# Two accumulator banks opened by real work, and the state tokens reordered so that one transfer stores 128 of them

## The chip, the cores and the metric

The kernel runs on one core of a Trainium2 chip. The metric is device time in microseconds (us) of one launch. A core has a matrix engine (TensorE, PE in the profile, its weight loads PEld), a vector engine (VectorE, DVE), a scalar engine (ScalarE, ACT), GpSimd (POOL) and SyncE (SP), which here only issues transfers. Each engine works through its own list of instructions in program order; semaphores tie the lists together. Matmul results land in PSUM, eight banks of 128 x 512 fp32.

## The reference

```python
# x: B=8, H=8, S=512, D=64; state: B, H, Ns=32, D; Dm = H*D = 512; E=8 experts, F=1024
a  = softmax(scale * x @ state.T);   xread = a @ state      # 512 rows per batch and head
a2 = softmax(scale * state @ x.T);   sread = a2 @ x         #  32 rows per batch and head
x  = concat([xread, sread], axis=2) -> (B*(S+Ns), H*D)      # 8 * 544 = 4352 tokens of 512
P  = exp(x @ w_gate - max);  8 times: P /= P.sum(1); P /= P.sum(0); P *= N / E
out = sum over e of P[:, e] * (relu(x @ w1[e]) @ w2[e])     # 4352 x 512, fp32
```

The order in which a kernel holds the tokens inside is free, as long as every row is stored at its place.

## The kernel before, in words

**Two stages.** Up to about 135 us the kernel computes the attention, expert 0, the gate and its eight normalisations, all as small operations whose order and engines stand in a list written out beforehand (PLAN, line 16, played by `issue`, line 105). After that a loop (lines 1039 to 1079) runs through experts 1 to 7. Both keep the running output in `acc`, 34 rows of 128 tokens x 512 columns in fp32.

**Token blocks.** Each expert has nine blocks: blocks 0 to 7 are the 512 x tokens of one batch, block 8 holds the 256 state tokens of all batches. `xsT` (line 165) holds the state tokens' inputs as 128 partitions x 4 chunks x 256 tokens; `keepS` (line 764) copies them there from PSUM, sixteen copies of 128 x 64, batch b at columns 32b to 32b+31. So a row of 128 state tokens in `acc` is four batches of 32, and `layer2_last` (line 299) stores it as four transfers of 32 rows, half of them from SP and half from ACT. The second of the two rows is computed in two halves of 256 columns.

**The loop.** One turn does layer 2 of a block (`layer2`, line 320) and, woven in, layer 1 of the next (`layer1`, line 263). Layer 2 is a seven-product scheme on a matrix cut in 2 x 2. The products go through PSUM in the order A, E, B, A, B, E, B, eight matmuls of 256 columns each; `add` (line 344) then puts a finished product into `acc`, weighted by P, as two DVE instructions of 128 x 256. The first A is also copied by ACT into the B bank (line 363), and the B products are added on top of it. The two B banks alternate from turn to turn. Layer 1 makes eight groups of 128 x 512 (two matmuls, line 255), which ACT passes through relu into `Hm` (line 275); after the fourth and the eighth group four DVE instructions form sums (lines 281 to 284), which the next turn's products read.

**Banks E and B also serve V.** For some turns, `project` (line 221) opens the turn with the V factors for later blocks: 24 small matmuls (line 235), the first into bank E and the turn's B bank. They wait until DVE has added what these banks held.

**The seeds.** In the first turn alone, `seed` (line 351) runs one matmul of 128 x 512 into each B bank, so that the later products, which never start a bank anew, add to it. What it writes is overwritten.

**The step counter.** `step` (line 1030) is called after each product and after each slot for a layer-1 group: 7 + 8 = 15 times a turn. Every sixth call advances `load_w` (line 188) by one, which first issues an expert's weight transfers and, 10 advances later, forms eight differences of its weights (line 206, eight DVE instructions of 128 x 512, called subs here), one at an advance. What is left of them when block 6 ends is emitted at once. So the position of a sub in DVE's list depends on the count alone; DVE's list is the program order of these calls.

**The turn's weighing.** Before the loop adds to `acc`, rows hold expert 0's unweighted result; `weigh` (line 292) multiplies a row by P. In the first turn, four rows are weighed on DVE, ACT, DVE and POOL.

Of the kernel before, what the change touches and what calls it, by code (L numbers as in the profile page):

```python
# [9 lines left out]
FP32 = mybir.dt.float32  # L10
FP16 = mybir.dt.float16
# [37 lines left out]
704V 689P 693P 690P 730P 398V 694A 399P 733P 731V 691A 732A 735A 734A 400V  # L49
""".split()  # L50
ENGINES = {"P": "PE", "V": "DVE", "A": "ACT", "G": "POOL", "D": "DMA", "S": "SPQ", "H": "HOST"}
NT_ = 2
ETX = 0
POOLB = 1
# [47 lines left out]
            slot.users.append(self)  # L102


def issue(ops):
    for step in PLAN:
        op = ops[int(step[:-1])]
        assert all(d.end for d in op.after) and ENGINES[step[-1]] in op.on
        for slot in op.takes:
            slot.ring.taken.append(slot)  # L110
            slot.tile = slot.make()
        op.emit(ENGINES[step[-1]])
        op.end = True
    assert all(op.end for op in ops) and len(PLAN) == len(ops)
# [3 lines left out]
def kernel(  # L118
# [9 lines left out]
    nc = tc.nc  # L128

    B, H, S, D = x.shape  # L130
# [30 lines left out]
    def bank(shape, dtype, name, tag="bank"):  # L161
        return pools[tag].tile(shape, dtype, name=name, tag=tag)
# [16 lines left out]
    w2r = moe_w2.rearrange("e (fb p) d -> e p fb d", p=128)  # L179

    outx = [out[b * SB:b * SB + S, :].rearrange("(p sc) d -> p sc d", sc=NSC) for b in range(B)]
    outs = out.rearrange("(b s) d -> b s d", s=SB)[:, S:, :]

    mw = ctx.enter_context(tc.tile_pool(name="moe_w", bufs=2))
    gsb = ctx.enter_context(tc.tile_pool(name="gate_sb", bufs=2))
# [72 lines left out]
    hid = {}  # L258
# [1 line left out]
    final = (E - 1, B)  # L260
    seeds = []

    def layer1(e, bi):

        t0, tn = blocks[bi]
        th = tn // 2
        Hm = hpool.tile([128, 2, NJ, S], FP16, name="Hm", tag="Hm")
        sm = hpool.tile([128, 3, NJ, S // 2], FP16, name="sm", tag="sm")
        hid[(e, bi)] = (Hm, sm)
        for j in range(NJ):  # L270
            for i in range(2):
                fb = i * NJ + j
                hps = bank([128, S], FP32, "hps", "h")
                hidden_ps(e, bi, fb, hps[:, :tn])
                nc.scalar.activation(out=Hm[:, i, j, :tn], in_=hps[:, :tn], func=AF.Relu)  # L275
                if j % 2 and i and (e, bi) != final:
                    def sums(jj=ds(j - 1, 2)):
                        a11, a21 = Hm[:, 0, jj, :th], Hm[:, 0, jj, th:tn]
                        a12, a22 = Hm[:, 1, jj, :th], Hm[:, 1, jj, th:tn]
                        s1, s2, s4 = (sm[:, k, jj, :th] for k in range(3))  # L280
                        nc.vector.tensor_add(s1, a21, a22)  # L281
                        nc.vector.tensor_sub(a21, a11, a21)  # L282
                        nc.vector.tensor_sub(s2, s1, a11)  # L283
                        nc.vector.tensor_sub(s4, a12, s2)  # L284

                    if DEFER and bi == 0 and j == 1:
                        late.append(sums)
                    else:
                        sums()
                yield  # L290
# [8 lines left out]
    def layer2_last():  # L299
        e, bi = final  # L300
        t0, tn = blocks[bi]
        Hm, _ = hid.pop(final)
        w2h = w16[e][1]
        nb = 128 // Ns
        for row in range(tn // 128):
            k = t0 // 128 + row
            parts = 1 + row
            for c in range(parts):
                cols = ds(c * (Dm // parts), Dm // parts)
                dst = bank([128, 512], FP32, "y", "AEh"[row + c])  # L310
                for fb in range(NFB):
                    nc.tensor.matmul(dst[:, :Dm // parts], Hm[:, fb // NJ, fb % NJ, ds(row * 128, 128)],  # L312
                                     w2h[:, fb, cols], start=(fb == 0), stop=(fb == NFB - 1))
                nc.vector.scalar_tensor_tensor(out=acc[:, k, cols], in0=dst[:, :Dm // parts], scalar=Pmat[:, k, e:e + 1],
                                               in1=acc[:, k, cols], op0=ALU.mult, op1=ALU.add)
            for i in range(nb):
                (nc.scalar if i % 2 else nc.sync).dma_start(
                    out=outs[row * nb + i], in_=acc[ds(i * Ns, Ns), k, :])

    def layer2(e, bi, n):  # L320
        t0, tn = blocks[bi]
        nk = tn // 256
        th = tn // 2
        Hm, sm = hid.pop((e, bi))
        w2h, T = w16[e][1], tsum[e]
        tb = t0 // 128
        p = Pmat[:, :, e:e + 1]
        A = bank([128, 2, DH], FP32, "A", "A")
        Eb = bank([128, 2, DH], FP32, "E", "E")

        def product(dst, lhs, rhs, first=False):
            for c in range(nk):
                for j in range(NJ):
                    nc.tensor.matmul(dst[:, c], lhs(j, c), rhs[:, j],  # L334
                                     start=first and c == 0 and j == 0, stop=(j == NJ - 1),
                                     skip_group_check=True)

        def h(i, half):
            return lambda j, c: Hm[:, i, j, ds(half * th + c * 128, 128)]

        def s(k):
            return lambda j, c: sm[:, k, j, ds(c * 128, 128)]

        def add(src, row, col):
            for c in range(nk):
                k = tb + row * nk + c
                dst = acc[:, k, ds(col * DH, DH)]
                nc.vector.scalar_tensor_tensor(out=dst, in0=src[:, c], scalar=p[:, k], in1=dst,  # L348
                                               op0=ALU.mult, op1=ALU.add)

        def seed(i):
            bb = bank([128, 2, DH], FP32, "Bseed", "B%d" % i)
            nc.tensor.matmul(bb.rearrange("p c d -> p (c d)"), identh, aT[:, 0, 0], start=True, stop=True)
            seeds.append(bb)

        if not n:
            for k, eng in enumerate(("DVE", "ACT", "DVE", "POOL")):
                weigh(k, eng)
        product(A, h(0, 0), w2h[:, :NJ, :DH], True)
        if not n:  # L360
            seed(0)
        Bb = seeds[n % 2]
        nc.scalar.copy(out=Bb[:, :nk], in_=A[:, :nk])  # L363
        yield
        product(Eb, s(0), T[:, 0], True)
        if not n:
            seed(1)
        add(Eb, 1, 1)
        yield
        product(Bb, s(1), T[:, 1])  # L370
        add(Bb, 0, 1)
        yield
        product(A, h(1, 0), w2h[:, NJ:, :DH])
        add(A, 0, 0)
        yield
        product(Bb, h(0, 1), T[:, 2])
        add(Bb, 1, 1)
        yield
        product(Eb, s(2), w2h[:, NJ:, DH:])
        add(Eb, 0, 1)  # L380
        yield
        product(Bb, h(1, 1), T[:, 3])
        add(Bb, 1, 0)
        if e == E - 1 and bi < B:
            for k in range(2 * nk):
                nc.sync.dma_start(out=outx[bi][:, k, :], in_=acc[:, tb + k, :])
        yield
# [179 lines left out]
    for b in range(B):  # L567
# [30 lines left out]
        for q in range(NQ):  # L598
# [163 lines left out]
                                             tile_position=(0, i * 64), skip_group_check=True)  # L762

            def keepS(eng, b=b, q=q, su=su):
                copy(eng, xsT[:, ds(2 * q, 2), ds(b * Ns, Ns)], su.tile)

            part("R%d" % (2 * b + q))
            u = op(r(9), {"PE": (0.26, 0.50)}, read, [k2], [su], [ETs, xn[b]])
# [246 lines left out]

                op((due_1 + 5.0 * bi, 2, j), {"DVE": (1.70, 1.85)}, sums, kept[-4:]).goal = -0.9

    issue(ops)
    for e in range(2):
        w16[e] = (wslots[e][0].tile, wslots[e][1].tile)  # L1020
    hpool = pools1["h"]
# [20 lines left out]
    for i, (e, bi) in enumerate(work):  # L1042
        if bi == 1 and e + 1 < E:
            wload.append(load_w(e + 1))
        if (e, bi) == final:
            layer2_last()
            break
        v, pat = iter(()), PATS if bi == B else PATN if bi == B - 1 else PAT0
        soon = work[:i + (3 if bi == B - 1 else 2)]
        need = sum(b < B for _, b in soon) * (F // 512)  # L1050
        if halves and all_halves - len(halves) < need:
            v, pat = project(halves[:SESSION], i), PATV
            del halves[:SESSION]
        if i:
            next(v, None)
        l2 = layer2(e, bi, i)
        l1 = layer1(*work[i + 1]) if i + 1 < len(work) and work[i + 1] not in hid else iter(())
        for k in range(7):
            next(l2)
            step()  # L1060
            if k == 0:
                next(v, None)
                next(v, None)
            if late:
                late.pop()()
            if e == 1 and bi < B and 3 <= k < 7:
                m = blocks[bi + 1][0] // 128 + k - 3
                if m < NTB:
                    weigh(m, "ACT")
            for _ in range(pat[k]):  # L1070
                next(l1, None)
                step()
        for part in (l1, l2):
            for _ in part:
                pass
        if bi == len(blocks) - 3:
            for _ in (x for w in wload for x in w):
                pass
            wload.clear()
# [30 lines left out]
```

## Time and profile before

| quantity | value |
|---|---|
| runs | 752.53, 752.74, 753.22 us; median 752.74 |
| profiled execution | 752.75 us, of which the span from first to last instruction is 751.0 |
| mean granted TensorE clock | 0.995 |
| busy PE / DVE / ACT / POOL | 736.0 / 617.0 / 517.7 / 70.8 us |
| seeds (line 353) | 2 matmuls, 379 ns each, at 136.0 and 137.3 us |
| subs (line 206) | 48 on DVE, about 415 ns each, from 191.0 to 649.6 us |
| stores of the state tokens (line 317) | 4 from SP, 4 from ACT, 64 KB each, issued from 746.1 to 748.0 us |

A matmul's time in the records overlaps the next one's: a run of matmuls of 512 columns starts one every 0.215 us, of 256 columns one every 0.109 us, whatever their own 0.38 and 0.27 us. In the timeline a line gives start, length, engine, source line, operation, result and operands, and how many instructions were merged; brackets hold the idle time before it.

### The profile page before, as it was taken

How to read it: one execution, taken by the hardware profiler on the slowest of the kernel's cores; microseconds unless marked ns; L12 is line 12 of the kernel's file. 1: busy time of each engine (PE TensorE's matmuls, PEld its weight loads, DVE VectorE, ACT ScalarE, POOL GpSimd, SP SyncE). 2: the span in 40 equal slices, each digit the busy share in tenths (PEclk: the TensorE clock that was granted, in tenths of full speed). 3: DMA queues.
4: the chain of work that ended last, by engine and by line, in shares of the span. 5: the costliest groups of instructions: out<-in, count | busy, mean ns of one | idle time of the engine just before them, and what ended most of it. 6: DMA issues, size and time to landing. Idle time of an engine off the chain costs nothing.

```text
span 751.0 us, 16151 instructions
## 1 busy us (share of the span) xinstructions
PE 736.0 (98%) x6517; PEld 502.2 (67%) x6517; DVE 617.0 (82%) x1529; ACT 517.7 (69%) x1014; POOL 70.8 (9%) x81
## 2 busy tenths in 40 slices
PE   5999999999999999999999999999999999999997
PEld 3444445666777777776776767776777767767776
DVE  5899989877888789788888788887897888887885
ACT  6876856799876766667666766667666676667662
POOL 4674410200010000100000000100001000000000
PEclk9899999999999999999999999999999999999999
DMA  9997560600033000700007000330007000002234
GB/s 179 140 134 131 82 99 1 109 6 1 1 61 53 2 1 2 113 1 2 1 2 112 2 1 1 58 57 1 1 2 112 2 1 2 1 31 94 103 113 141
DMA packets 51323, 36.71 MB, mean 49 GB/s; under 512 B 25392, under 2 KB 43824, under 8 KB 51248
## 3 DMA queue, kind: packets, MB, share of 16 engines
q0 software_dynamic: 22272, 20.97, 18.5%
q1 hardware_dynamic: 27744, 14.18, 7.6%
q8 instruction: 51, 0.84, 0.5%
q10 hardware_dynamic: 1232, 0.52, 0.3%
q14 instruction: 24, 0.20, 0.1%
HBM read 42.48 MB, written 8.91 MB: 68 GB/s over the span
## 4 chain that ended last, share of the span: by engine, by line
PE 92%; DVE 3%; DMA 1%; ACT 1%; POOL 1%; issue 0%; SPq 0%; POOLq 0%; DVEq 0%; ACTq 0%
PE hps L255 28%; PE Bseed L334 20%; PE A L334 14%; PE E L334 14%; PE yps L935 6%; PE hps L897 4%; PE v_ps L235 4%; DMA xT<-x_nat 1%; DMA x_nat<-in_x_dram 1%; PE y L312 0%; PE v_ps L870 0%; POOL a L670 0%; ACT Hm L275 0%; DVE acc L348 0%; POOL E L662 0%; PE su_ps L758 0%
## 5 line engine op out<-in xcount | busy, mean ns | idle before, releaser
L275 ACT ACTIVATE Hm<-hps 128x512 f16<-128x512 f32 (+1 forms) x496 | 265.8, 577 | 130.5 <-PE hps L255 128.1
L255 PE MATMUL hps<-aT,V 128*128 128x512 f16 x880 | 230.6, 379 | 0.0
L334 PEld LDWEIGHTS <-Hm 128*128 128x128 f16 x1888 | 181.6, 98 | 71.3 <-issue 15.9
L348 DVE SCALAR_TENSOR_TENSOR acc<-Bseed,Pmat,acc 128x256 f32<-128x256 f32 x354 | 155.0, 477 | 9.8 <-PE Bseed L334 6.9
L334 PEld LDWEIGHTS <-sm 128*128 128x128 f16 x1416 | 138.3, 98 | 34.5 <-issue 0.3
L334 PE MATMUL A<-w2h,Hm 128*128 128x256 f16 x944 | 123.7, 273 | 0.0
L334 PE MATMUL Bseed<-T,Hm 128*128 128x256 f16 x944 | 123.3, 273 | 0.0
L255 PEld LDWEIGHTS <-V 128*128 128x128 f16 x880 | 86.1, 98 | 50.8
L348 DVE SCALAR_TENSOR_TENSOR acc<-E,Pmat,acc 128x256 f32<-128x256 f32 x236 | 103.2, 476 | 13.8 <-PE E L334 13.5
L281 DVE TENSOR_TENSOR sm<-Hm 128x512 f16<-128x512 f16 (+1 forms) x122 | 50.1, 411 | 60.4 <-ACT Hm L275 60.2
L243 ACT CAST V<-v_ps 128x512 f16<-128x512 f32 x144 | 74.2, 612 | 0.0
L348 DVE SCALAR_TENSOR_TENSOR acc<-A,Pmat,acc 128x256 f32<-128x256 f32 x118 | 51.9, 479 | 17.9 <-PE A L334 17.6
L935 PE MATMUL yps<-w2h,hT 128*128 128x512 f16 x272 | 64.1, 379 | 0.1
L334 PE MATMUL E<-w2h,sm 128*128 128x256 f16 x472 | 61.7, 273 | 0.0
L334 PE MATMUL E<-T,sm 128*128 128x256 f16 x472 | 61.6, 273 | 0.0
L334 PE MATMUL Bseed<-T,sm 128*128 128x256 f16 x472 | 61.5, 272 | 0.0
L363 ACT COPY Bseed<-A 128x512 f32<-128x512 f32 (+1 forms) x62 | 34.1, 550 | 37.9 <-PE A L334 35.3
L282 DVE TENSOR_TENSOR Hm<-Hm 128x512 f16<-128x512 f16 (+1 forms) x122 | 50.3, 412 | 4.2
L284 DVE TENSOR_TENSOR sm<-Hm,sm 128x512 f16<-128x512 f16 (+1 forms) x122 | 50.2, 412 | 4.2
L283 DVE TENSOR_TENSOR sm<-sm,Hm 128x512 f16<-128x512 f16 (+1 forms) x122 | 49.4, 405 | 0.0
L194 POOL DMA_DIRECT2D w1h<-in_moe_w_dram x12 | 8.5, 714 | 396.9 <-PE hps L255 396.5
L935 PEld LDWEIGHTS <-hT 128*128 128x128 f16 x272 | 25.4, 99 | 28.9 <-issue 1.8
(127 smaller groups left out, 617.7 us busy)
## 6 DMA issues: line engine op xcount, KB each, us to landing
w1h<-in_moe_w_dram POOLq DMA_DIRECT2D x16, 512.0 KB, 7.0
w2h<-in_moe_w_dram POOLq DMA_DIRECT2D x16, 512.0 KB, 8.4
out_dram<-acc SPq DMA_DIRECT2D x32, 256.0 KB, 2.5
x_nat<-in_x_dram POOLq DMA_DIRECT2D x16, 256.0 KB, 5.6
st_st<-in_state_dram ACTq DMA_DIRECT2D x1, 256.0 KB, 4.9
st_st<-in_state_dram SPq DMA_DIRECT2D x1, 256.0 KB, 4.2
ETs<-E SPq DMA_TRANSPOSE x16, 4.3
out_dram<-acc SPq DMA_DIRECT2D x4, 64.0 KB, 1.8
```

The lines of the kernel that those rows point to most:

```text
L235: nc.tensor.matmul(ps[q][ds(j * Ns, Ns), :], stT[ds(r, 64), bi, q, ds((j ^ q) * Ns, Ns)], w1h[ds(r, 64), 2 * q + j // 2, cols], tile_posit ...
L243: nc.scalar.copy(out=dst, in_=src)
L255: nc.tensor.matmul(out, lhs, rhs, start=(k == 0), stop=(k == len(terms) - 1))
L275: nc.scalar.activation(out=Hm[:, i, j, :tn], in_=hps[:, :tn], func=AF.Relu)
L281: nc.vector.tensor_add(s1, a21, a22)
L282: nc.vector.tensor_sub(a21, a11, a21)
L283: nc.vector.tensor_sub(s2, s1, a11)
L284: nc.vector.tensor_sub(s4, a12, s2)
L334: nc.tensor.matmul(dst[:, c], lhs(j, c), rhs[:, j], start=first and c == 0 and j == 0, stop=(j == NJ - 1), skip_group_check=True)
L348: nc.vector.scalar_tensor_tensor(out=dst, in0=src[:, c], scalar=p[:, k], in1=dst, op0=ALU.mult, op1=ALU.add)
L363: nc.scalar.copy(out=Bb[:, :nk], in_=A[:, :nk])
L935: nc.tensor.matmul(yps.tile, hT[fb].tile[:, ds(tk * 128, 128)], w2h[:, fb, :], start=(fb == 0), stop=(fb == NFB - 1))
```

## The change

1. **First turn.** The seed matmuls go. Both B banks are allocated ahead of the turn. Layer 2 gets an extra stop after its first product, at which the first layer-1 group of the next block runs, into the B bank of this turn instead of a bank of its own (`lent`); relu empties it, and then the copy of A goes into it. The other B bank is first written by the V matmuls of the second turn. The rows are weighed in another order (2 on DVE, 3 on POOL, 0 on DVE, 1 on ACT behind the copy). The extra stop calls `step` once more.
2. **State tokens.** `keepS` writes batch b at every fourth column, so that a row of 128 tokens has the batch innermost; `layer2_last` stores the first row by one transfer (SP), and each half of the second row by one as soon as it is added (ACT, then SP).
3. `issue` gets a hook, `idle`, whose table `IDLE` is empty: nothing is emitted.

```diff
-    outs = out.rearrange("(b s) d -> b s d", s=SB)[:, S:, :]
+    nb = 128 // Ns
+    outs = out.rearrange("(g b s) d -> g s b d", b=nb, s=SB)[:, S:, :, :]
@@ layer1(e, bi, lent=None)
-                hps = bank([128, S], FP32, "hps", "h")
+                if lent is None:
+                    hps = bank([128, S], FP32, "hps", "h")
+                else:
+                    hps, lent = lent, None
@@ layer2_last
-            for i in range(nb):
-                (nc.scalar if i % 2 else nc.sync).dma_start(
-                    out=outs[row * nb + i], in_=acc[ds(i * Ns, Ns), k, :])
+                (nc.scalar if c + 1 < parts else nc.sync).dma_start(
+                    out=outs[row, :, :, cols], in_=acc[:, k, cols])
@@ layer2
-        def seed(i):
-            bb = bank([128, 2, DH], FP32, "Bseed", "B%d" % i)
-            nc.tensor.matmul(bb.rearrange("p c d -> p (c d)"), identh, aT[:, 0, 0], start=True, stop=True)
-            seeds.append(bb)
-
         if not n:
-            for k, eng in enumerate(("DVE", "ACT", "DVE", "POOL")):
+            for k, eng in ((2, "DVE"), (3, "POOL"), (0, "DVE")):
                 weigh(k, eng)
         product(A, h(0, 0), w2h[:, :NJ, :DH], True)
+        Bb = seeds[n % 2]
         if not n:
-            seed(0)
-        Bb = seeds[n % 2]
+            yield
         nc.scalar.copy(out=Bb[:, :nk], in_=A[:, :nk])
+        if not n:
+            weigh(1, "ACT")
         yield
         product(Eb, s(0), T[:, 0], True)
-        if not n:
-            seed(1)
         add(Eb, 1, 1)
@@ keepS
-                copy(eng, xsT[:, ds(2 * q, 2), ds(b * Ns, Ns)], su.tile)
+                copy(eng, xsT.rearrange("p c (g n b) -> p c g n b", g=B // nb, b=nb)[:, ds(2 * q, 2), b // nb, :, b % nb], su.tile)
@@ the loop
+        if not i:
+            seeds += [bank([128, 2, DH], FP32, "Bseed", "B%d" % k) for k in range(2)]
         l2 = layer2(e, bi, i)
-        l1 = layer1(*work[i + 1]) if i + 1 < len(work) and work[i + 1] not in hid else iter(())
+        l1 = iter(())
+        if i + 1 < len(work) and work[i + 1] not in hid:
+            l1 = layer1(*work[i + 1], None if i else seeds[0].rearrange("p c d -> p (c d)"))
+        if not i:
+            next(l2)
+            next(l1)
+            step()
         for k in range(7):
             next(l2)
             step()
```

More of the change, by code (lines that the diff above doesn't have):

```diff
@@ L51 @@
 ENGINES = {"P": "PE", "V": "DVE", "A": "ACT", "G": "POOL", "D": "DMA", "S": "SPQ", "H": "HOST"}
+IDLE = {}
 NT_ = 2
@@ L102, in __init__, with issue @@
             slot.users.append(self)
-def issue(ops):
+def issue(ops, idle):
     for step in PLAN:
@@ L111, in issue @@
             slot.tile = slot.make()
+        idle(op.takes[0].tile if op.takes else None, IDLE.get(int(step[:-1]), 0))
         op.emit(ENGINES[step[-1]])
@@ L261, with layer1 @@
     seeds = []
-    def layer1(e, bi):
+    def layer1(e, bi, lent=None):
         t0, tn = blocks[bi]
@@ L303, in layer2_last @@
         w2h = w16[e][1]
-        nb = 128 // Ns
         for row in range(tn // 128):
@@ L1016, with idle @@
                 op((due_1 + 5.0 * bi, 2, j), {"DVE": (1.70, 1.85)}, sums, kept[-4:]).goal = -0.9
-    issue(ops)
+    def idle(t, n):
+        if not n:
+            return
+        t = t.rearrange({2: "p a -> p a", 3: "p a b -> p (a b)", 4: "p a b c -> p (a b c)"}[len(t.shape)])[:, :128]
+        for _ in range(n):
+            if t.dtype == FP16:
+                nc.tensor.transpose(t, identh, identh)
+            else:
+                nc.tensor.matmul(t, identh, identh, start=True, stop=True, skip_group_check=True)
+    issue(ops, idle)
     for e in range(2):
```

## The prediction

> **What bounds the kernel now.** The page comes first: engines, then the chain that ended last.
>
> ```profile
> PE 736.0 (98%) x6517; PEld 502.2 (67%) x6517; DVE 617.0 (82%) x1529; ACT 517.7 (69%) x1014; POOL 70.8 (9%) x81
> ...
> PE 92%; DVE 3%; DMA 1%; ACT 1%; POOL 1%; issue 0%; SPq 0%; POOLq 0%; DVEq 0%; ACTq 0%
> ```
>
> PE bounds it: a matmul removed is time gained, and so is a wait of PE. But DVE at 82% over all hides a tight place in every turn, which the timeline shows. First a turn (expert 2, block 2) without a sub, then one (expert 5, block 5) with a sub of line 206 before the second E adds:
>
> ```profile
> 252.25 0.87 DVE L348 SCALAR_TENSOR_TENSOR acc<-Bseed,Pmat,acc 128x256 f32<-128x256 f32 x2
> 253.04 0.87 DVE L348 SCALAR_TENSOR_TENSOR acc<-E,Pmat,acc 128x256 f32<-128x256 f32 x2
> 253.19 1.04 PE L334 MATMUL Bseed<-T,Hm 128*128 128x256 f16 x8
> 254.93 0.28 PE L334 MATMUL A<-w2h,Hm 128*128 128x256 f16 x1
> ```
> ```profile
> 546.24 0.87 DVE L348 SCALAR_TENSOR_TENSOR acc<-Bseed,Pmat,acc 128x256 f32<-128x256 f32 x2
> 547.02 0.41 DVE L206 TENSOR_TENSOR T<-w2h 128x512 f16<-128x512 f16 x1
> 547.16 1.04 PE L334 MATMUL Bseed<-T,Hm 128*128 128x256 f16 x8
> 547.36 0.87 DVE L348 SCALAR_TENSOR_TENSOR acc<-E,Pmat,acc 128x256 f32<-128x256 f32 x2
> 549.05 1.05 PE L334 MATMUL A<-w2h,Hm 128*128 128x256 f16 x8
> ```
>
> The last B product starts 0.07 us after the B adds end (252.25 + 0.87 = 253.12), in the second turn 0.05: it overwrites what they read, and there is no slack. The sub puts the E adds off by 0.34 (547.36 - 547.02). The V matmuls behind the product need bank E empty, and so the next A starts 1.89 us after the last B product instead of 1.74.
>
> The first turn and the end, from the timeline:
>
> ```profile
> 135.14 1.05 PE L334 MATMUL A<-w2h,Hm 128*128 128x256 f16 x8
> 136.03 0.38 PE L353 MATMUL Bseed<-aT,identh 128*128 128x512 f16 x1
> 136.41 1.03 PE L334 MATMUL E<-T,sm 128*128 128x256 f16 x8
> 136.86 0.60 ACT L363 COPY Bseed<-A 128x512 f32<-128x512 f32 x1
> 137.28 0.38 PE L353 MATMUL Bseed<-aT,identh 128*128 128x512 f16 x1
> 137.93 1.04 PE L334 MATMUL Bseed<-T,sm 128*128 128x256 f16 x8
> ```
> ```profile
> 746.06 2.33 ACTq L317 DMA_DIRECT2D out_dram<-acc  x4
> 747.02 0.48 DVE L314 SCALAR_TENSOR_TENSOR acc<-y,Pmat,acc 128x256 f32<-128x256 f32 x1 [0.39 <-PE y L312]
> ```
> ```profile
> out_dram<-acc SPq DMA_DIRECT2D x32, 256.0 KB, 2.5
> ...
> out_dram<-acc SPq DMA_DIRECT2D x4, 64.0 KB, 1.8
> out_dram<-acc ACTq DMA_DIRECT2D x4, 64.0 KB, 2.0
> ```
>
> **Part 1, the seeds: -0.43.** Two matmuls of 512 columns go, 2 x 0.215 = 0.43 us of PE. The layer-1 group that comes forward is done once either way. What it risks is the copy: relu and copy now run one after the other before the first B product. The group starts where the seed did, 136.03, and ends by 136.62 (0.59, as line 255's pairs take); ACT is free at 136.35, its V casts done; relu 136.66 to 137.26, copy 137.29 to 137.88 (0.60 each), product at 137.93: the same moment as before, with a group more behind it. The V factors that it reads come from the first ACT cast, done about 135.3, and the DVE cast, 135.31. Nearest bounds: -0.25 if relu and copy come 0.18 later, -0.60 if the gap of 0.17 ahead of E (136.41 against 136.03 + 0.215) goes with no wait in its place. The weighing is covered: E's second add waits for POOL's row 3 until 138.05 as before; row 1, now behind the copy, is ready about 138.6, its adds come at 139.1. On ACT the next relu waits behind it until 138.6 instead of 138.19, and four layer-1 banks cover that. The fourth relu comes one place earlier, so the first turn's sums do too, and its last B product, 0.43 earlier, finds its bank free. The second bank needs no work: 24 V matmuls write it in the second turn anyway (145.41).
>
> **Part 2, the extra step: +1.87.** The first turn calls `step` 16 times instead of 15, and from then on every sub stands one place earlier in DVE's list. PE's list is otherwise untouched. By letters (adds E, B, A; sums S; sub T), the order in which the instructions stand is:
>
> ```
> expert, block   before        after          expert, block   before        after
> 1, 5            EBTASBTESB    ETBASTBESTB    4, 5            EBATSBETSB    EBATSBTESB
> 1, 6            TEBATSBETSB   EBTASBTESB     4, 6            ETBASBTESB    ETBASTBESTB
> 2, 5            EBATSBETSB    EBATSBTESB     5, 5            EBTASBTESB    ETBASTBESTB
> 2, 6            EBTASBTESB    ETBASTBESTB    5, 6            TEBATSBETSB   EBATSBTESB
> 3, 5            ETBASBTESB    ETBASTBESTB    6, 5            EBATSBETSB    EBTASBTESB
> 3, 6            TEBATSBETSB   EBATSBTESB     6, 6            EBTASBTESB    ETBASTBESTB
> ```
>
> - New is the pair S T B, a sub between the first sums and the second B adds, once an expert. No turn before has it. From the sums' start DVE runs without a pause (sums, B, E), so the sub's 0.34 goes onto the B adds, and the last B product waits for them. Slack, from the timeline: 0.01 to 0.02 where V matmuls opened the turn (253.19 against 253.12, less the 0.05 that is always there), 0.08 where not (340.69 against 340.56), none in expert 1, where ACT's weighing already keeps that product waiting (196.14; its layer-1 matmuls end at 195.19 + 0.86 = 196.05). So 0.34 (expert 1), 3 x 0.33 (experts 2, 5, 6), 2 x 0.27 (3, 4): 1.87.
> - T before the E adds costs only where V matmuls open the next turn: last B product to next A took 1.74 without (340.69 to 342.43), 1.83 with it (371.14 to 372.97), and 1.89 in the turn shown. Before, four turns pay: 3,5 and 4,6 0.09 each, 5,5 and 6,6 0.15 each, 0.48. After, these are S T B turns, where V starts later by more than the E adds do, and four others pay: 1,6 and 6,5 0.09, 2,5 and 3,6 0.15: 0.48 again. No change.
> - Subs at other places (B T A, A T S, E T B) lie in DVE's idle time: 0.36 us before the A adds, 1.16 before the sums.
> - Bounds: 0 if the sub slips in unseen, as those do; 2.35 if each S T B costs a sub's whole 0.42 less the slack (0.42 + 3 x 0.41 + 2 x 0.35). I take the 0.34 measured between the very neighbours B, T, E. POOL's list is unchanged, and the weight transfers are issued long before they are read.
>
> **Part 3, the end: -0.35.** Before, the last adds end at 747.50 (747.02 + 0.48); then each queue issues two transfers, the last from ACT at 748.0 with 2.0 us to landing, 750.0; 1.0 more to the span's end. After, one transfer of 128 KB follows the adds, from SP at 747.57. No row has 128 KB: between 1.8 (64 KB) and 2.5 (256 KB). By size 2.0; I take 2.1, since its runs are 1 KB: 749.65, -0.35. Bounds: -0.6 (1.8) and +0.1 (2.5). The first half's transfer leaves ACT about 746.7 and has landed by then. The Trainium skill speaks against such a gain: "DMA: Bandwidth & Descriptors", Anatomy of one DMA, gives 2.0 us fixed plus the bytes at 436 GB/s, here 2.3 us as an estimate. By that the part would bring 0.1 and the sum would be 754.1; the rows of 1.8 for 64 KB lie below the rule.
>
> **Part 4, the strided copies: 0.** Sixteen `keepS` copies of about 0.21 us now write every fourth element. Nearest row: the DVE reduction that reads its 272 values strided takes 0.65 against 0.44 in a row, +0.05 for 64 values. They end by 98.7 us; only the last two lead on, through the gate to P at 136.1, and the bank that waits for P's first adds is not written again for 4 us. So 0 to +0.3, and I take 0.
>
> **Sum.** 752.75 - 0.43 + 1.87 - 0.35 = 753.84, about 753.8. The profiled execution is within 0.01 of the median 752.74.
>
> **Rivals.**
> - *The sub stays hidden (ends faster).* If S T B costs the last B product nothing, because the sums start earlier than the rows say, only the gains are left: 752.75 - 0.43 - 0.35 = 751.97, and to 751.6 with the better bounds. It decides if the sum of the S T B waits is under 0.78. For it: the B, T, A and A, T, S subs do vanish. Against: the sums wait for ACT's relu, which nothing moves, and the slack was read as 0.01 to 0.08.
> - *The gains fail.* The copy keeps PE waiting at the first turn (-0.25), the last transfer lands like one of 256 KB (+0.1), a sub costs 0.42 at its six places (2.35): 752.75 - 0.25 + 0.1 + 2.35 = 754.95. For it: no row shows these sizes. Against: three bounds together.
> - *The change does not do what it says.* The list of PE shows both seeds gone, that of SP and ACT three stores instead of eight. There is no room for this one.
>
> **How the numbers follow.** Forecast, each part near its price: 0.66, 753.2 to 754.7. Sub hidden: 0.15, 751.3 to 752.8. Gains fail: 0.19, 754.3 to 755.3. The range 752.2 to 755.0 takes in the forecast, most of the third case and half of the second. A measurement here tells 0.2%, 1.5 us, from no change: 751.2 and 754.2. Above 754.2 lie the third case and a quarter of the forecast, 0.35; under 751.2 the tail of the second and what I overlook, 0.06; between them 0.59.
>
> **What would show it.** No line 353; the first B product still near 137.9; the next turn's V matmuls near 145.0 instead of 145.41. In the six S T B turns, a wait of PE for DVE of 0.27 to 0.34 ahead of the last B product, and the new line of subs between sums and B adds; these turns, from first A to next first A, 10.7 to 10.8 us long where V matmuls follow and 9.9 to 10.0 where not. The last store landing about 749.65 plus the shift. Wrong if these turns keep their length, if the last transfer takes 2.5 or more, or if anything before 135 us moves by more than 0.3.

## The result, and the profile after

The changed kernel takes 755.09 us (median of 17 runs, 753.66 to 756.85) where the kernel before takes 752.97 us (17 runs, 751.01 to 755.71): a ratio of 1.0026, 95% interval 1.0018 to 1.0034. On the 752.74 us of the forecast that ratio is 754.7 us. The forecast was 753.8, in a range of 752.2 to 755.0: a loss, as forecast, but nearly twice as large (+1.96 us instead of +1.09), and, with 0.26% (interval from 0.18%), past the 0.2% within which I had put the likeliest outcome.

When the first turn starts differs from run to run: two kernels with the same first part (the changed kernel, and the one without the extra step below) start it at 134.16 and at 135.77 us. So the prediction's sign of being wrong, that anything before 135 us moves by more than 0.3 us, tells nothing here. Two profiles are therefore compared from the first A product of the loop to the span's end, called the stretch here. It takes 615.83 us before (750.97 - 135.14) and 617.73 us after (751.89 - 134.16): +1.90, which is the difference in time within its interval (1.4 to 2.6 us). Turns are numbered from 0: turn n is expert 1 + n // 9, block n % 9.

The page of the changed kernel, its engines and the chain that ended last:

```profile
PE 735.7 (98%) x6515; PEld 501.1 (67%) x6515; DVE 616.8 (82%) x1529; ACT 518.6 (69%) x1014; POOL 70.7 (9%) x81
...
PE 88%; DVE 5%; ACT 3%; DMA 2%; POOL 1%; issue 0%; SPq 0%; POOLq 0%; ACTq 0%
```

PE has two matmuls fewer, and yet its share of the chain falls from 92% to 88%: DVE and ACT now stand where PE stood. This shift belongs to the moved subs: with the extra step alone the shares are 88% PE, 5% DVE and 3% ACT, and without it 92, 3 and 1%. A share of the chain is not the loss, which is 0.3% of the span. The costliest groups show two new waits of PE (busy time, mean ns, idle time ahead and what ended it), first after, then before:

```profile
L338 PE MATMUL Bseed<-T,Hm 128*128 128x256 f16 x944 | 123.3, 273 | 1.0 <-DVE acc L352 0.8
...
L338 PE MATMUL Bseed<-T,sm 128*128 128x256 f16 x472 | 61.6, 272 | 0.3
```
```profile
L334 PE MATMUL Bseed<-T,Hm 128*128 128x256 f16 x944 | 123.3, 273 | 0.0
...
L334 PE MATMUL Bseed<-T,sm 128*128 128x256 f16 x472 | 61.5, 272 | 0.0
```

The later B products (from `Hm`) now wait 1.0 us for DVE's adds, as forecast. The first B products (from `sm`) wait 0.3 us, which was not. Both are counted from the modelled ends of the matmuls ahead and so are too small; the lengths of the turns below have the whole of it. The timeline of the S T B turn of expert 5, block 5 (turn 41), whose counterpart of before the prediction shows:

```profile
546.46 0.42 DVE L209 TENSOR_TENSOR T<-w2h 128x512 f16<-128x512 f16 x1
546.52 1.03 PE L258 MATMUL hps<-aT,V 128*128 128x512 f16 x4
546.79 0.87 DVE L352 SCALAR_TENSOR_TENSOR acc<-Bseed,Pmat,acc 128x256 f32<-128x256 f32 x2
...
547.72 1.03 PE L338 MATMUL Bseed<-T,Hm 128*128 128x256 f16 x8 [0.17 <-DVE acc L352]
```

The sub stands between sums and B adds and puts them off by 0.33 (546.79 - 546.46). The four layer-1 matmuls, one every 0.215, are done at 547.38; the product starts at 547.72, 0.06 after the adds: a wait of 0.34. The turn takes 10.77 us instead of 10.59, because the next A came late before too (the E adds behind the sub). The first turn, in the same view:

```profile
134.16 1.05 PE L338 MATMUL A<-w2h,Hm 128*128 128x256 f16 x8
...
135.05 0.59 PE L258 MATMUL Bseed<-aT,V 128*128 128x512 f16 x2
...
135.68 0.60 ACT L281 ACTIVATE Hm<-Bseed 128x512 f16<-128x512 f32 x1 [0.30 <-PE Bseed L258]
...
136.31 0.57 ACT L362 COPY Bseed<-A 128x512 f32<-128x512 f32 x1
...
136.93 1.03 PE L338 MATMUL Bseed<-T,sm 128*128 128x256 f16 x8
```

The first B product starts 2.77 us after the first A (2.79 before), with a layer-1 group already done, and the next turn's V matmuls start 9.81 after it (143.97) instead of 10.27. The end, timeline and then the transfers (KB each, median us to landing):

```profile
747.99 0.48 DVE L319 SCALAR_TENSOR_TENSOR acc<-y,Pmat,acc 128x256 f32<-128x256 f32 x1 [0.39 <-PE y L317]
```
```profile
out_dram<-acc ACTq DMA_DIRECT2D x1, 128.0 KB, 2.3
out_dram<-acc SPq DMA_DIRECT2D x1, 128.0 KB, 2.1
```

SP finds the last store landed 2.15 us after the adds end at 748.47, where it was 2.46 before: 0.3 us gained. But the span ends 3.42 after the adds, and did so 3.46 after them before. All turns whose length differs by more than 0.05 us between the two profiles, first A to next first A:

| turn (expert, block) | before | after | difference |
|---|---|---|---|
| first turn (1,0) | 11.04 | 10.59 | -0.45 |
| S T B: 1,5 / 2,6 | 9.67 / 9.58 | 10.00 / 9.90 | +0.33, +0.32 |
| S T B: 3,5 / 4,6 / 5,5 / 6,6 | 10.52 / 10.52 / 10.59 / 10.58 | 10.70 / 10.70 / 10.77 / 10.77 | +0.18, +0.18, +0.18, +0.19 |
| T before the last E adds: 1,6 / 2,5 / 3,6 / 6,5 | 10.43 / 10.45 / 10.45 / 10.43 | 10.52 / 10.59 / 10.59 / 10.52 | +0.09, +0.14, +0.14, +0.09 |
| turns 29 (4,2) and 56 (7,2), without a sub | 9.58 / 9.58 | 9.86 / 9.87 | +0.28, +0.29 |

First turn -0.45, subs +1.84, turns 29 and 56 +0.57, the end -0.04; a few hundredths are rounding. Turns 29 and 56 have no sub and no moved instruction. In turn 29 the timeline shows what is late:

```profile
420.19 1.05 PE L338 MATMUL A<-w2h,Hm 128*128 128x256 f16 x8
...
421.61 0.57 ACT L362 COPY Bseed<-A 128x512 f32<-128x512 f32 x1 [0.65 <-PE A L338]
...
422.23 1.03 PE L338 MATMUL Bseed<-T,sm 128*128 128x256 f16 x8
```

The same turn before:

```profile
420.42 1.05 PE L334 MATMUL A<-w2h,Hm 128*128 128x256 f16 x8
...
421.56 0.57 ACT L363 COPY Bseed<-A 128x512 f32<-128x512 f32 x1 [0.36 <-PE A L334]
...
422.18 1.03 PE L334 MATMUL Bseed<-T,sm 128*128 128x256 f16 x8
```

ACT's copy of A starts 1.42 us after the A product does, 1.14 before, and the B product waits for it. In the trace's records ACT's semaphore wait ahead of the copy ends at 421.29, with the A product; the copy follows after 0.32 us, where this usually takes 0.04. Counted from 0 in ACT's records, semaphore waits included, the copy stands at place 703 of ACT's list in turn 29 and at 1087 in turn 56. Both leave 63 on division by 128. Before they stood at 704 and 1088: the new first turn has one semaphore wait fewer on ACT.

### The profile page after: what moved, and what is told of

It reads as the page before. It is cut to its first block, busy times and chain, and to the rows that moved or that the text cites. A ratio compares the mean times of both kernels' runs of the same rounds, so it can differ in the third digit from the quotient of the medians.

```text
span 751.9 us, 16140 instructions
## 1 busy us (share of the span) xinstructions
PE 735.7 (98%) x6515; PEld 501.1 (67%) x6515; DVE 616.8 (82%) x1529; ACT 518.6 (69%) x1014; POOL 70.7 (9%) x81
## 4 chain that ended last, share of the span: by engine, by line
PE 88%; DVE 5%; ACT 3%; DMA 2%; POOL 1%; issue 0%; SPq 0%; POOLq 0%; ACTq 0%
PE hps L258 26%; PE Bseed L338 20%; PE A L338 14%; PE E L338 12%; PE yps L934 6%; PE hps L896 4%; PE v_ps L238 4%; ACT Hm L281 2%; DMA xT<-x_nat 1%; DVE acc L352 1%; DMA x_nat<-in_x_dram 1%; PE su_ps L757 0%; PE y L317 0%; DVE sm L287 0%; DVE Hm L288 0%
```

## The experiments

Two theories stood against each other. Mine: the loss is the place of the subs, 1.84 us, plus 0.57 us for ACT's place in its list, while the stores' gain is used up behind the landing. The rival: the subs are hidden, and stores and first turn cost what is seen. All numbers below that are not ratios come from the profiles, one execution of each kernel.

| kernel | ratio to before (95%) | stretch, us | last adds to span's end, us |
|---|---|---|---|
| before | | 615.83 | 3.46 |
| after | 1.0026 (1.0018 to 1.0034) | 617.73 | 3.42 |
| without the extra step | 0.9994 (0.9983 to 1.0006) | 615.85 | 3.38 |
| extra step alone | 1.0030 (1.0017 to 1.0043) | 617.66 | 3.46 |
| tokens and stores alone | 1.0000 (0.9990 to 1.0010) | 615.77 | 3.41 |
| one more ACT instruction | 1.0020 (1.0009 to 1.0030) | 617.13 | 3.39 |
| 18 S T B pairs | one run, no ratio | 620.88 | 3.41 |
| six more stores | 1.0019 (1.0008 to 1.0031) | 617.32 | 3.02 |
| 128 / 101 / 86 more on ACT | one run each, no ratio | 617.68 / 617.73 / 617.16 | 3.42 / 3.41 / 3.42 |
| best of the parts | 0.9988 (0.9978 to 0.9997) | 614.50 | 3.05 |

**Without the extra step.**

```diff
             next(l2)
             next(l1)
-            step()
```

> The changed kernel without the additional step() in the first turn: subs stand where they stood before the change, everything else is the changed kernel's. All numbers from the first A product to the span's end (615.86 us before, 617.74 us after). Theory (the place of the subs costs 1.84 us): no S T B turn is left and the stretch shrinks by 1.84 us against the changed kernel, to about 615.9 us; the first turn stays at 10.6 us. Rival (the pairs S T B wait in the place of something else, and the loss comes from the new stores and the first turn): the stretch stays near 617.7 us. About turns 29 and 56, which are 0.28 us longer in the changed kernel: if ACT's position in its list does it, they stay 0.28 us longer, since ACT's list is the changed kernel's; if the moved subs do it, both go back to 9.58 us and the stretch is 615.3 us.

The stretch is 615.85 us, 1.88 less than in the changed kernel; all ten turns with subs have the lengths of before, the first turn stays at 10.59, turns 29 and 56 at 9.86 and 9.87. In turn 41 the sub is behind the B adds again (timeline):

```profile
546.68 0.87 DVE L352 SCALAR_TENSOR_TENSOR acc<-Bseed,Pmat,acc 128x256 f32<-128x256 f32 x2
...
547.46 0.41 DVE L209 TENSOR_TENSOR T<-w2h 128x512 f16<-128x512 f16 x1
547.61 1.04 PE L338 MATMUL Bseed<-T,Hm 128*128 128x256 f16 x8
```

The product no longer waits. One call, which adds no work, costs as much as the whole net loss; what is left of the other parts cancels (first turn -0.45, turns 29 and 56 +0.57, end -0.08). And since turns 29 and 56 are late without the moved subs, these are not their cause.

**The extra step alone.**

```diff
 # kernel before
-    n = 0
+    n = 1
```

> The kernel before with its step counter started at 1, so that every sub stands one place earlier, as in the changed kernel; the seeds, the token order and the stores are as before. Theory: six S T B turns, 0.18 us longer (three times, V matmuls next), 0.32 to 0.34 us longer (twice and once), four turns of 10.5 to 10.6 us take the places of four others, together +1.84 us: from the first A product to the span's end 617.7 us against 615.86 us. Rival (S T B is hidden without the other parts): 615.9 us. About turns 29 and 56: if ACT's position in its list makes them longer, they stay at 9.58 us here (ACT's list is that of the kernel before); if the moved subs do, both are 0.28 us longer and the stretch is 618.3 us.

617.66 us, +1.83, with the changed kernel's lengths in all ten turns (one 0.01 off) and 9.58 in turns 29 and 56. The place of the subs costs its 1.84 with the old first turn and the old stores just as well.

**Tokens and stores alone.** The kernel before with the new `keepS`, `outs` and `layer2_last` only.

```diff
-                copy(eng, xsT[:, ds(2 * q, 2), ds(b * Ns, Ns)], su.tile)
+                copy(eng, xsT.rearrange("p c (g n b) -> p c g n b", g=B // nb, b=nb)[:, ds(2 * q, 2), b // nb, :, b % nb], su.tile)
...
-            for i in range(nb):
-                (nc.scalar if i % 2 else nc.sync).dma_start(
-                    out=outs[row * nb + i], in_=acc[ds(i * Ns, Ns), k, :])
+                (nc.scalar if c + 1 < parts else nc.sync).dma_start(
+                    out=outs[row, :, :, cols], in_=acc[:, k, cols])
```

> The kernel before with the state tokens in the new order and the three stores alone; seeds, first turn and subs as before. Theory (the last store lands 0.33 us sooner, but SP then still steps through six semaphores at about 0.06 us each, where it stepped through one or two): from the last adds' end to the span's end 3.43 us against 3.50 us before, the stretch from the first A product 615.8 us, and the start of that stretch as far as runs scatter (0.3 us or more). Rival A (the end is worth the 0.35 us that I forecast): 615.5 us. Rival B (the strided copies of the tokens delay the first part): the stretch starts up to 0.3 us later than in runs of the kernel before.

3.41 us from the adds to the end: 0.05 gained, not 0.35. The loop starts at 135.07, within the scatter of the starts, and the ratio is 1.0000 within 0.1%: a cost of the strided copies above 0.75 us is excluded, a smaller one isn't resolved.

**One more ACT instruction.** The tiny activation that loads ACT's table, issued twice.

```diff
-lambda _: nc.scalar.activation(out=warm, in_=warm, func=AF.Exp), ops[-1:])
+lambda _: [nc.scalar.activation(out=warm, in_=warm, func=AF.Exp) for _ in range(2)], ops[-1:])
```

> The changed kernel with the tiny activation that loads ACT's table issued twice, so that all of ACT's list from there on stands one instruction later, as in the kernel before. Theory (turns 29 and 56 are 0.28 us longer because ACT's copy of A into B stands last in a block of 128 instructions of ACT's list, at 703 and 1087, and starts 0.28 us late there): both go back to 9.58 us and the stretch from the first A product to the span's end is 617.74 - 0.57 = 617.2 us. Rival (the data, the subs or the transfers at those times do it): both stay at 9.86 us and the stretch at 617.7 us.

Both turns are back at 9.58 us, and the stretch is 617.13, 0.60 less, with one instruction more. Turn 29 in the timeline:

```profile
420.49 1.05 PE L338 MATMUL A<-w2h,Hm 128*128 128x256 f16 x8
...
421.63 0.57 ACT L362 COPY Bseed<-A 128x512 f32<-128x512 f32 x1 [0.36 <-PE A L338]
...
422.25 1.03 PE L338 MATMUL Bseed<-T,sm 128*128 128x256 f16 x8
```

**128, 101 and 86 more.** Is it the place on division by 128, or would any shift do? Tiny copies behind the activation move all of ACT's list; the first part starts later by what they take (first A at 158.62, 156.66 and 149.68 us), which says nothing of the loop.

```diff
+[nc.scalar.activation(out=warm, in_=warm, func=AF.Exp)] + [nc.scalar.copy(out=warm, in_=warm) for _ in range(128)]
```

> The changed kernel with 128 additional tiny copies on ACT behind the activation that loads its table, so that all of ACT's list stands 128 instructions later; the first part starts later by what they take. Theory (the position in blocks of 128 instructions makes turns 29 and 56 longer): 128 is a whole block, so both turns are 9.86 us again, as in the changed kernel, and unlike with one additional instruction. Rival (any shift, or any delay of the first part, takes the 0.28 us away): both are 9.58 us.

> The changed kernel with 101 additional tiny copies on ACT ahead of the first part. In the changed kernel ACT's copies of A into B in turns 31 and 58 stand at 730 and 1114 of its list; here at 831 and 1215, both 63 on division by 128, with the semaphore wait at 62. Theory (a copy at 63, behind a semaphore wait at 62, starts 0.28 us late): turns 31 and 58 are 0.28 us longer than in the changed kernel, and turns 29 and 56 are back at 9.58 us. In turns 22 and 49 the copy stands at 65 here; by the theory they stay at 9.58 us, and a longer time there would say that the place is wider. Rival (turns 29 and 56 have something else of their own, such as a transfer at that time): they stay at 9.86 us, and 31 and 58 do not change.

> As the run with 101 additional copies, with 86: the copies of turns 14 and 41 then stand at 62 on division by 128 (574 and 958) with their semaphore wait at 61, those of turns 32 and 59 at 65, and none with a semaphore wait ahead of it at 63 or 64. Theory in its narrow form (only a copy at 63 is late): no turn is longer than in the changed kernel, and turns 29 and 56 are back at 9.58 us. Rival (the block's refill delays whatever stands just ahead of it): turns 14 and 41 are 0.28 us longer too.

With 128 more, turns 29 and 56 take 9.86 again. With 101 they take 9.58, and turns 31 and 58 take 10.72 instead of 10.44, with the copy 1.42 us after A once more (timeline of turn 31):

```profile
462.72 1.05 PE L338 MATMUL A<-w2h,Hm 128*128 128x256 f16 x8
...
464.14 0.57 ACT L362 COPY Bseed<-A 128x512 f32<-128x512 f32 x1 [0.65 <-PE A L338]
...
464.76 1.03 PE L338 MATMUL Bseed<-T,sm 128*128 128x256 f16 x8
```

Turns 22 and 49, at place 65, keep their 9.58. With 86 no turn is longer, though copies stand at 62 (turns 14 and 41) and at 65 (32 and 59). So for this copy it is place 63 alone, and only behind a separate semaphore wait: in the changed kernel's turns 20 and 47 no copy is late at 62, and in the kernel before one stands at 63 there with nothing ahead of it but an activation, and is not late. For other instructions the place is not enough: with 101 and with 86 more, two relus each stand at 63 directly behind a separate wait (575 and 959, 703 and 1087) and start 0.04 us after it, as usual.

**18 S T B pairs.** The dose: the same subs, three S T B turns an expert instead of one.

```diff
-        if n % 6 == 0 and wload:
+        if n % 5 == 3 and wload:
...
-            step()          # the one added in the first turn
```

> The changed kernel without the additional step(), and with the sub issued on every step() whose count leaves 3 on division by 5 (instead of every sixth): the 8 subs of an expert then stand in three turns, each of which has one pair S T B; 18 such pairs instead of the changed kernel's six, and no sub before the last E adds. Theory (each pair costs the 0.27 to 0.34 us by which the last B product waits): against the kernel without the additional step() 18 x 0.27 to 18 x 0.34 less the 0.48 us that its other subs cost, +4.4 to +5.6 us; from the first A product to the span's end 620.2 to 621.4 us. Rival (only the first such pair after a weight transfer costs, or the pairs cost by something else than their place): 617.7 us or less.

620.88 us: 5.03 above the kernel without the extra step, or 0.31 us a pair ((5.03 + 0.48) / 18). Its row of later B products, beside 1.0 in the changed kernel:

```profile
L338 PE MATMUL Bseed<-T,Hm 128*128 128x256 f16 x944 | 123.3, 273 | 2.8 <-DVE acc L352 2.1
```

**Six more stores.** Where does the gain of the earlier landing go? In the trace's records SP, once all is issued, steps through nine waits for transfers, always in the same order, and about 0.06 us apart when nothing holds it. The transfers take eight of these semaphores in turn. The changed kernel's last store has the third wait of the list. SP passes it at 750.62, and six more up to 750.98; before, the last store to land had the seventh (749.97).

```diff
-                nc.sync.dma_start(out=outx[bi][:, k, :], in_=acc[:, tb + k, :])
+                for c in ([ds(0, DH), ds(DH, DH)] if bi < 3 and k < 2 else [ds(0, Dm)]):
+                    nc.sync.dma_start(out=outx[bi][:, k, c], in_=acc[:, tb + k, c])
```

> The changed kernel with six of the x stores of the first three blocks of the last expert split into two halves each, some 80 us ahead of the end: six more transfers, so that the last store's semaphore is the last of SP's list instead of the third. Theory (after the landing SP steps through six more semaphores at 0.06 us each): the landing stays 2.1 us after the issue, and from the last adds' end to the span's end it is 3.42 - 0.36 = 3.06 us. Rival (the order does not matter, the stretch behind the landing is fixed): 3.4 us as in the changed kernel. Everything else as in the changed kernel.

3.02 us instead of 3.42: the last store's wait is now the last of the list. SP passes it at 751.12, 2.08 us after the store's issue (2.09 in the changed kernel), and the span ends 0.88 later instead of 1.26. The waits of SP at the end (us in all, times, longest), first in the changed kernel, then here:

```profile
SPq L1122 <- DMA out_dram<-acc: 1.4, 2, 0.7
```
```profile
SPq L1123 <- DMA out_dram<-acc: 1.0, 2, 0.7
```

The last landing holds SP 0.7 us in both; what comes behind it is what differs. Six transfers more made the end 0.4 us sooner in the profile; the ratios (1.0019 and 1.0026) are too close to show it.

**Best of the parts.** The changed kernel without the extra step, with subs at `n % 5 == 2`, one more ACT instruction and the six split stores.

```diff
-        if n % 6 == 0 and wload:
+        if n % 5 == 2 and wload:
```

> The seeds, the token order and the stores of the changed kernel, without the additional step(), with the sub on every step() whose count leaves 2 on division by 5 (pairs B T A... become A T S and E T S, all in DVE's idle time), one additional tiny ACT instruction, and the six split x stores. Theory, against the kernel before, from the first A product to the span's end: first turn -0.45, subs -0.48, end -0.40, turns 29 and 56 unchanged, together -1.33: 614.5 us, a ratio of 0.9982. Rival (E T S delays the sums and with them the last B product, as S T B did): no gain of 0.48 and up to 0.3 us for each of 18 turns, 615 to 620 us.

614.50 us, and 0.9988 in time (0.9978 to 0.9997): faster than both kernels. No turn waits for a sub, those with V matmuls behind them are at 10.43 to 10.45 (10.53 and 10.54 in expert 1, blocks 1 and 4, against 10.53 in both before), and the chain that ended last is PE's again:

```profile
PE 94%; DMA 2%; DVE 2%; ACT 1%; POOL 1%; issue 0%; SPq 0%; POOLq 0%; ACTq 0%
```

E T S does not delay the sums, since DVE waits there 1.16 us for ACT's relu in any case.

## Why the prediction was right or wrong

- **Part 1, the seeds: right at its place (-0.45 for -0.43), but not all of the part.** That ACT's list gets one instruction shorter, and what this does 290 and 550 us later, was not in it. The prediction went through what the first turn's instructions do there; of every later turn it took for granted that ACT's copy starts as before. +0.57, from the two runs that move ACT's list alone (shift of one: gone; shift of 128: back), and the two that move it elsewhere. With it the first turn's change is worth +0.12, no gain.
- **Part 2, the extra step: right, turn by turn.** +1.84 for +1.87, S T B turns at 9.90 to 10.00 and 10.70 to 10.77, T before the E adds no net change (0.46 for 0.48). The rival that the sub stays hidden is refuted by the run with the step alone, and by the dose.
- **Part 3, the end: the term that was mis-sized.** "749.65, -0.35" was right up to the landing: 2.1 us for 128 KB from SP as taken, and 0.3 earlier. But "1.0 more to the span's end" was carried over from before as if it were fixed. It is 1.26 after, since six waits follow the store's own instead of two; the end is worth -0.04. That 2.1 came out was partly luck: the reason given, runs of 1 KB, is not borne out: the twelve split x stores of the run with six more stores, 128 KB each and also in runs of 1 KB, took 1.86 to 2.02 us to land. The Trainium skill's "DMA: Bandwidth & Descriptors", Anatomy of one DMA, from which the prediction worked out 2.3 us, gives its fit for transfers that GpSimd issues; these stores are issued by SP (2.07) and ACT (2.25), so the fit was no price for them. What decided was behind the landing.
- **Part 4, the strided copies: 0 stands**, as far as 0.1% can tell. The copies themselves take longer, 288 ns instead of 209 on DVE and 316 instead of 226 on ACT: 0.08 to 0.09 us each, where the prediction had worked out 0.05.
- **The sum:** 1.09 forecast, + 0.57 (ACT's place) + 0.31 (the end) - 0.05 (seeds and subs) = 1.92, for 1.90 seen. The rival "the gains fail" named about the right total for wrong reasons: the copy did not keep PE waiting, the transfer did not land like one of 256 KB, and a sub did not cost 0.42.
- **The chances:** with the two unseen terms the likeliest case would have lain above 0.2%. It was priced as if only the lines of the diff could change the time. That 754.7 still lies in the range is luck: the room up to 755.0 was left for the gains failing together, not for these two terms.

## What to carry to other kernels

Before a counter or a generator is called once more, list what else it paces: here a call without work of its own moved 48 vector instructions by one place, and the six that came to stand between the sums and the adds that empty a bank cost more (1.84 us) than the change could gain. A price for the end of a kernel runs to the last instruction, not to the landing: look at which wait of the closing list the last transfer has. And where turns without any moved instruction change by a few tenths of a us, compare the places of the late instructions in their engine's list before looking for a cause in the data.

## What the runs showed of the hardware

- **A late copy at one place in 128.** In every loop position tried, ACT's copy of A at place 63 on division by 128, behind a separate semaphore wait, started 0.32 to 0.33 us after the wait instead of 0.04 (turns 29 and 56, or 31 and 58 when the list is moved by 101); at 62, 64 and 65 it did not. Places are counted from ACT's first record; where the chip's own blocks begin, the trace does not say. The trace has transfers of 8192 bytes on a queue of kind "instruction" at about these places: at 422.26, when ACT had begun place 704, and likewise near 447, 574, 831, 958 and 1089, that is every 128 instructions. In the kernel with one more ACT instruction that of turn 29 starts at 421.23, while ACT still waits for A; in the changed kernel only 0.97 us after the wait has ended. So the request for the next instructions lies behind the wait in one case and not in the other. It also lies ahead of the four relus at 63 that are not late, by about 6.5 us. But with 86 more, the copies at 62 have it 1.0 us behind their wait and are not late. That the request itself is what delays the copy was not measured.
- The Trainium skill's "Runtime: NRT & Kernel Launch", Instruction fetch mechanics, has the sequencer fetch its own instructions in blocks of 256 while it executes, and calls the cost of a boundary mostly hidden. The transfers at ACT's places here come every 128 instructions. Nearly all of them show no cost; the 0.28 us of turns 29 and 56 would be an exception, if the request is the cause.
- **The closing list.** SP's nine waits cost about 0.06 us each, whether their transfers have landed long ago or not, and always in the same order. The last transfer's place in it therefore depends on how many transfers went before: third in the changed kernel, last with six more.
- **Issue.** The three new stores, each writing 128 rows of 1 or 2 KB with the batch innermost, take 0.54 to 0.67 us to issue, the eight of before 0.31 to 0.43 us each. The split x stores, 128 rows of 1 KB in plain order, take 0.33 to 0.42, so it is not the number or the size of the rows.
